# Block-sparse attention for the last two head pairs of a fused attention and gated-MLP kernel, with sampled keys copied by GpSimd and sampled value rows gathered by DMA

## The chip, the cores and the metric

The kernel runs on one core of a Trainium2 chip. The metric is the device time of one execution in microseconds, lower being better. Engines are named as in the profile: PE is TensorE, DVE is VectorE, ACT is ScalarE, POOL is GpSimd, SP is SyncE.

## The reference

BigBird attention over 4 batches, 8 heads, 768 tokens and 64 features, in blocks of 32 tokens (24 blocks), and then a gated MLP over the 512 features of each batch.

```python
mask = np.abs(blk_i - blk_j) <= 1                     # neighbours
mask |= (blk_i == 0) | (blk_j == 0) | (blk_i == 23) | (blk_j == 23)
for qb in range(24):
    for kb in sampled_blocks[qb]:                     # 3 drawn blocks, may repeat
        mask[qb*32:(qb+1)*32, kb*32:(kb+1)*32] = True
attn = softmax(where(mask, q @ k.T / 8, -1e9));  x = attn @ v
...
h = relu(x @ w_in);  u, v = halves of h
v_n = (v - mean(v)) / sqrt(var(v) + 1e-6)
out = (u * (w_spatial @ v_n + b_spatial)) @ w_out     # w_spatial mixes tokens
```

A query block thus attends to at most 8 of the 24 key blocks (itself, its neighbours, the first, the last, three drawn), except the first and last query blocks, which attend to all. The drawn blocks are an input, known only when the kernel runs.

## The kernel before, in words

Heads go in pairs; the four pairs of a batch fill the 128 partitions of four feature tiles. There are 16 pairs, numbered 0 to 15. The work is written out by hand as a sequence of slots, and no scheduler changes the order: every engine executes its instructions in program order. Functions put into a slot by `when` (line 726) are called in the loop at line 846.

Pairs 0 to 3 (batch 0) are treated in thirds in slots 0 to 35. From slot 36 on (`S0`) each head takes six slots and each pair twelve; `slot_of(p)` is the first. Pair 14 begins at slot 156 and pair 15 at 168; the last dense slot is 179.

- **Loads** (`load`, line 106) bring q, k and v of a pair, each partition holding six consecutive tokens, through SyncE's queue. **Casts** (`cast`, line 118) to bf16 are done on GpSimd. **`tr_dma`** (line 373) transposes q and k by a DMA from SyncE, and **`split`** (line 376) copies a head's half into `kq` on VectorE, beside rows that carry the block mask.
- **`qk_full`** (line 421): scores of 128 keys by all 768 queries, two matmuls (512 and 256 columns, line 428) per slot, and one exponential on ScalarE (line 431) into `a_all`. The mask comes in through 24 extra rows of the contraction, so all 24 x 24 blocks are computed.
- **`av_full`** (line 471): seven slots later, six matmuls of 65 columns (line 476) sum value rows of 128 queries; column 65 is the sum of weights. `normalize` (line 438) divides on VectorE.
- **`xtr_dma`** (line 507) transposes a pair's result into `xt`, the input of the MLP. For the last pair `last_x` (line 785) does it on PE, behind all that is left of the MLP of batch 2.

The **MLP** of a batch is cut into 108 steps of about one 512-column matmul (lines 561 and 630). `deal` and `run_queue` spread them evenly over 48 slots; those of batch 2 run in slots 144 to 191, that is beside pairs 13 to 15, and those of batch 3 behind everything. Six v products come first, mixed with the u products: for each, VectorE takes the relu (line 185), the statistics (lines 594 and 595), and after three of them GpSimd works out `std` and `rstd` (lines 598 and 600). Nine or more steps later VectorE normalizes `vn` in place (`vn_one`, line 615, recorded as line 185). From about slot 165 on the spatial products (line 630, `w_spt` by `vn`) read all six `vn`, and VectorE multiplies the result into `un` (lines 661 and 664). PSUM gives the MLP two banks, the scores two tiles and the values two.

SyncE issues every DMA of this stage in program order, output stores among them, and waits at one whose data aren't ready.

## Time and profile before

| | |
|---|---|
| median of 3 runs | 210.07 us (209.88 to 210.24) |
| span of the profiled execution | 208.3 us |
| time of the profiled execution around its span | not given; the median is 1.77 us above the span |
| PE, DVE, ACT, POOL busy | 201.0, 146.8, 168.4, 89.4 us |
| DMA | 39.48 MB, all on hardware queues |

A profile row names line, engine and operation, then the tile written and the tile read, the shape, and how many there were. "PEld" is a weight load. In the grouped view the columns are busy time and mean duration of one in ns, then the idle time ahead of it and who ended it; in the timeline the first two numbers are start and length in us, and the bracket tells idle time ahead and its releaser. Matmuls are pipelined, so durations of single matmuls overlap.

### The profile page before, as it was taken

Reading aid. Unit: us, or ns where it says so; the run is one execution under the profiler, and the core shown is the slowest. Engines: PE = TensorE matmul, PEld = TensorE weight load, DVE = VectorE, ACT = ScalarE, POOL = GpSimd, SP = SyncE. Lnnn points to the kernel's source line nnn. Section 1 sums busy time; section 2 is a strip of 40 time slices with the busy share of each in tenths; the row PEclk is TensorE's granted clock in tenths of the full one; section 3 lists DMA queues with packets and bytes.
Section 4 is the critical chain, followed back from the end, with each engine's and each line's share of the span. In section 5 each row is a group of like instructions: output and inputs, shape, how many; then the busy total and the mean of one; then the engine's idle time right before and its main releaser. Section 6 shows DMA issues by size and latency. Waiting matters only on the chain.

```text
span 208.3 us, 5489 instructions
## 1 busy us (share of the span) xinstructions
PE 201.0 (97%) x2203; PEld 138.0 (66%) x2225; DVE 146.8 (70%) x315; ACT 168.4 (81%) x222; POOL 89.4 (43%) x186
## 2 busy tenths in 40 slices
PE   6899999999999999999999999999999999999993
PEld 6599888777766776667556676667665567445551
DVE  6888776989876766575975585456875666576871
ACT  6899999999999999989899878889899884266021
POOL 6888989767927964006757600006210000013000
PEclk9999999999999999999999999999999999999999
DMA  5999899999999999499987920499402010610016
GB/s 143 338 362 357 275 383 270 206 247 389 253 253 308 259 300 208 139 199 386 292 176 206 139 41 0 164 189 335 75 0 41 0 37 4 250 57 0 0 70 232
DMA packets 53053, 39.48 MB, mean 190 GB/s; under 512 B 33956, under 2 KB 47652, under 8 KB 53028
## 3 DMA queue, kind: packets, MB, share of 16 engines
q1 hardware_dynamic: 52596, 38.74, 70.0%
q10 hardware_dynamic: 432, 0.39, 0.6%
q8 instruction: 17, 0.28, 0.5%
q14 instruction: 8, 0.07, 0.1%
HBM read 24.77 MB, written 6.29 MB: 149 GB/s over the span
## 4 chain that ended last, share of the span: by engine, by line
PE 87%; DVE 4%; ACT 4%; DMA 2%; issue 1%; POOL 0%; ACTq 0%
PE ps L428 21%; PE ps_moe L630 17%; PE ps_moe L561 13%; PE ps_av L476 12%; PE ps L415 7%; PE ps_av L458 4%; PE ps_t L561 4%; PE ps_t L630 4%; PE ps_sc L630 2%; ACT a_all L420 2%; DVE stats L594 2%; DVE vn L185 2%; DMA st_q<-in_q_dram 2%; PE ps_sc L561 1%; PE ps L263 1%
## 5 line engine op out<-in xcount | busy, mean ns | idle before, releaser
L431 ACT ACTIVATE a_all<-ps 128x768 bf16<-128x768 f32 x144 | 113.4, 812 | 13.8 <-PE ps L428 6.2
L428 PE MATMUL ps<-kq 128*128 128x512 bf16 (+1 forms) x288 | 70.3, 326 | 0.3
L476 PEld LDWEIGHTS <-a_all 128*128 128x128 bf16 x864 | 46.6, 98 | 19.0
L476 PE MATMUL ps_av<-vv,a_all 128*128 128x65 bf16 x864 | 51.1, 194 | 0.1
L428 PEld LDWEIGHTS <-kq 128*128 128x128 bf16 x288 | 27.9, 97 | 23.6
L137 POOL CAST nat<-st_k 128x256 bf16<-128x256 f32 (+3 forms) x37 | 17.7, 509 | 38.7 <-DMA st_k<-in_k_dram 38.7
L420 ACT ACTIVATE a_all<-ps 128x1024 bf16<-128x1024 f32 x35 | 33.5, 1027 | 0.3
L630 PE MATMUL ps_moe<-w_spt,vn 128*128 128x512 bf16 (+1 forms) x144 | 33.1, 325 | 0.0
L598 POOL TENSOR_SCALAR std<-mv 128x3 f32<-128x3 f32 (+1 forms) x9 | 3.4, 376 | 48.7 <-DVE mv L595 48.5
L661 DVE TENSOR_TENSOR sb<-ps_moe,b_row 128x512 f32<-128x512 f32 x18 | 12.4, 690 | 14.5 <-PE ps_moe L630 14.2
L630 PE MATMUL ps_moe<-xt,w_in_t 128*128 128x256 bf16 (+1 forms) x108 | 21.7, 299 | 0.2
L415 PE MATMUL ps<-kq 128*128 128x256 bf16 x135 | 20.8, 275 | 0.8 <-DVE kq L211 0.6
L561 PE MATMUL ps_moe<-w_in_t,xt 128*128 128x512 bf16 x65 | 20.2, 378 | 0.2
L137 POOL CAST vv<-st_v 128x256 bf16<-128x256 f32 (+2 forms) x37 | 18.5, 533 | 3.9 <-DMA st_v<-in_v_dram 3.8
L137 POOL CAST nat<-st_q 128x256 bf16<-128x256 f32 (+2 forms) x41 | 19.2, 496 | 1.6 <-DMA st_q<-in_q_dram 1.5
L561 PE MATMUL ps_moe<-w_out_t,un 128*128 128x512 bf16 x64 | 19.4, 378 | 0.2
L441 DVE TENSOR_TENSOR xn<-ps_av,rc 128x384 bf16<-128x384 f32 (+1 forms) x36 | 18.5, 513 | 1.4 <-DVE rc L440 0.2
L664 DVE TENSOR_TENSOR un<-sb,un 128x512 bf16<-128x512 f32 x24 | 17.4, 727 | 1.5
L630 PEld LDWEIGHTS <-vn 128*128 128x128 bf16 x192 | 15.5, 97 | 4.4
L594 DVE BATCH_NORM_STATS2 stats<-vn 128x6 f32<-128x512 bf16 x24 | 16.5, 688 | 1.5 <-ACT vn L589 0.9
L211 DVE COPY osb<-ps_moe 128x512 f32<-128x512 f32 x12 | 8.3, 689 | 11.2 <-PE ps_moe L561 9.3
L211 DVE COPY kq<-tt 64x1536 bf16<-64x1536 bf16 x24 | 15.4, 641 | 0.6 <-DMA tt<-nat 0.2
(94 smaller groups left out, 241.6 us busy)
## 6 DMA issues: line engine op xcount, KB each, us to landing
out_dram<-osb SPq DMA_DIRECT2D x23, 256.0 KB, 2.1
st_k<-in_k_dram SPq DMA_DIRECT2D x15, 384.0 KB, 4.6
st_v<-in_v_dram SPq DMA_DIRECT2D x15, 384.0 KB, 6.2
st_q<-in_q_dram SPq DMA_DIRECT2D x12, 384.0 KB, 4.9
ws_f<-in_moe_w_spatial_dram SPq DMA_DIRECT2D x6, 384.0 KB, 5.5
w_f<-in_moe_w_in_dram SPq DMA_DIRECT2D x8, 256.0 KB, 6.3
w_f<-in_moe_w_out_dram SPq DMA_DIRECT2D x4, 256.0 KB, 5.4
st_q<-in_q_dram SPq DMA_DIRECT2D x3, 256.0 KB, 6.9
```

Source lines behind the costliest of these rows:

```text
L137: eng.tensor_copy(out=dst, in_=src)
L211: nc.vector.tensor_copy(out=o, in_=i)
L415: nc.tensor.matmul(out=ps[:, at:at + n * TW], lhsT=kq[:, h, ci * 128:(ci + 1) * 128], rhs=kq[:, h, qcols(t0, n)], start=True, stop=True)
L420: nc.scalar.activation(out=out, in_=ps, func=AF.Exp, scale=0.125)
L428: nc.tensor.matmul(out=ps[:, n0:n1], lhsT=kq[:, j % H, ci * 128:(ci + 1) * 128], rhs=kq[:, j % H, S + n0:S + n1], start=True, stop=True)
L431: nc.scalar.activation(out=a_ref["h", j][:, ci, :], in_=ps[:, 0:S], func=AF.Exp, scale=0.125)
L441: nc.vector.tensor_tensor(out=out, in0=ps[:, :, 0:D], in1=rc[:, 0:n].to_broadcast([128, n, D]), op=ALU.mult)
L476: nc.tensor.matmul(out=av_ref[j][:, qc, :], lhsT=a_ref["h", j][:, ci, qc * 128:(qc + 1) * 128], rhs=vv[p % NVV][:, h, ci, :], start=(ci == ...
L561: nc.tensor.matmul(out=ref["ps"][:, 0:w], lhsT=lhs(i), rhs=rhs(i), start=(i == 0), stop=(i == n - 1))
L594: nc.vector.bn_stats(out=stats, in_=self.vn[:, tcc, :])
L630: nc.tensor.matmul(out=o.rearrange("p (c t) -> p c t", c=n), lhsT=lhs(i)[:, (d0 + x) * 128:(d0 + x + 1) * 128], rhs=rhs(i), start=(i == 0) ...
L664: nc.vector.tensor_tensor(out=self.in_place(*area), in0=sb, in1=self.in_place(*area), op=ALU.mult)
```

## The change

Pairs 14 and 15 (`PS = NP - 2`) leave the dense path. Line numbers of the changed kernel are given where needed.

**Data.** q, k and v of the two pairs are loaded with token t on partition t mod 128 (runs of 256 bytes, one DMA per head), so that transposed columns are tokens in order. Their bf16 value rows, 260 wide for four heads, are also written to a scratch tensor in memory with 32 zero rows behind them.

**Keys.** For query blocks 3 to 22 two blocks share a chunk "f" of 128 keys: the two blocks themselves, the first and the last. Each query block has a chunk "x": one neighbour outside of the pair, and its three drawn blocks. Blocks 1 and 2 form one more such group, blocks 0 and 23 use all keys ("d"). VectorE copies fixed keys (`k_pairs`, `k_edges`); GpSimd copies drawn ones (`k_sampled`), loading twelve block positions at a time into registers.

**Values.** Fixed rows come by plain DMAs (`v_pairs`); for each x chunk one indirect DMA from GpSimd fetches 128 rows (`v_sampled`). Repeated or already present blocks are pointed at the zero rows, by an index computed on GpSimd (`sample_index`, about 45 small operations).

**Attention.** Per pair 17 score matmuls of 128 columns (chunks f and d, two heads at once) and 22 of 64 (x), nine exponentials, and 78 value matmuls. Weights go into 128x128 tiles that are zero outside the chunk's own queries; VectorE sets `a_cols` to zero once for that (`a_zero`). Queries are turned by 96 tokens (`q_split`), and results turned back by `x_order`. Value matmuls follow scores by four slots in place of seven.

```diff
+    def k_sampled(x0, n):
+        vals = nc.values_load_multi_w_load_instructions(
+            key_at[0:1, x0:x0 + n].rearrange("o n r -> o (n r)"),
+            engines=[mybir.EngineType.Pool], min_val=0, max_val=S - BLK,
+            skip_runtime_bounds_check_because="block numbers")[1]
+        src = kt_cols.rearrange("x (i t) -> x i t", i=2)
+        for j, val in enumerate(vals):
+            x, r = x0 + j // NR, j % NR
+            nc.gpsimd.tensor_copy(out=xk[:, :, x, (r + 1) * BLK:(r + 2) * BLK],
+                                  in_=src[:, :, bass.ds(val, BLK)])
+    def v_sampled(x):
+        nc.gpsimd.indirect_dma_start(
+            out=vx(x), out_offset=None, in_=rows_of_v,
+            in_offset=bass.IndirectOffsetOnAxis(ap=row_at[:, x:x + 1], axis=0))
+    def a_zero(n, eng):
+        eng.memset(a_cols[:, n * AW:min((n + 1) * AW, A_END)].bitcast(FP32), 0.0)
+    def q_split(i, h, copy):
+        rs = slice(h * D, (h + 1) * D)
+        src = tt["q"].rearrange("x c n -> x (c n)")[rs, i * S:(i + 1) * S]
+        copy(q2[i][rs, h, 0:S - QR], src[:, QR:S])
+        copy(q2[i][rs, h, S - QR:S], src[:, 0:QR])
+    def scores(ps, at, i, kind, n):
...
+        w = BLK if kind == "x" else 2 * BLK
+        nc.tensor.matmul(out=ps[:, at:at + 2 * w].rearrange("p (h t) -> p h t", h=2),
+                         lhsT=lhs, rhs=q2[i][:, :, t0:t0 + w], start=True, stop=True)
...
-    for p in range(NG, NP):
+    for p in range(NG, PS):
...
+    T = slot_of(PS)
+    when(70, samples)
...
+    for i in range(80, 100):
+        when(i, lambda: [todo.pop(0)() for _ in range(min(2, len(todo)))])
+    when(100, zero_rows)
+    when(101, v_ones, c(q_zero, 0), c(q_zero, 1))
+    for nm, p, ld, ca in (("v", 14, 110, 122), ("v", 15, 114, 124), ("k", 14, 116, 127),
+                          ("k", 15, 118, 129), ("q", 14, 126, 138), ("q", 15, 136, 146)):
+        when(ld, c(load, p, nm))
+        when(ca, c(cast, p, nm, PL))
+    when(126, v_out)
+    when(131, c(tr_group, "k"))
+    when(134, v_pairs)
+    for i in range(2):
+        when(136 + i, c(k_edges, i, dve_copy))
+        when(140 + 2 * i, c(k_pairs, i, dve_copy))
+    for x in range(NX):
+        when(134 + x, c(v_sampled, x))
+    for j in range(6):
+        when(137 + 3 * j, c(k_sampled, 4 * j, 4 if j < 5 else 2))
+    when(148, c(tr_group, "q"))
+    for i in range(2):
+        for h in range(2):
+            when(152 + 4 * i + h, c(q_split, i, h, dve_copy))
+    when(T - 5, c(a_zero, 0, nc.vector))
+    when(T + 2, c(a_zero, 1, nc.vector))
+    when(T + 7, c(a_zero, 2, nc.vector))
...
-    for s in range(NS + LAG + 2):
+    for s in range(NS + LAG):
```

In the slots, `samples` and the index operations (two a slot) come early, then four fills of 64x768 on GpSimd (`q_zero`), 22 gathers, 66 copies in six groups, and the three fills `a_zero` of 2304, 2304 and 384 words on VectorE; `T` is slot 156.

The `tr_dma` and `split` calls of pairs 14 and 15 are gone, with their four copies of 64x1536 on VectorE. `last_x` moves from slot 188 to 186; its two copies on VectorE become one there and two on ScalarE. The MLP's staging tiles `osb` go from 6 to 5, and several tiles now share one space. In GpSimd's program order the gathers and copies stand in six groups, each of three or so gathers and up to twelve copies; the two query casts lie behind the first and the third group, and the first `std` and `rstd` of batch 2 stand behind 19 of the gathers and all 66 copies. In VectorE's order the first normalization of `vn` stands ahead of the last `q_split`, two v products and two of the three `a_zero`.

327 lines of the change are left out of this document (302 added, 25 removed).

## The prediction

> **What bounds the kernel now.** I read the page first, for which engine is full, then the chain, then the stage that the change touches.
>
> ```profile
> span 208.3 us, 5489 instructions
> PE 201.0 (97%) x2203; PEld 138.0 (66%) x2225; DVE 146.8 (70%) x315; ACT 168.4 (81%) x222; POOL 89.4 (43%) x186
> ...
> PEclk9999999999999999999999999999999999999999
> ...
> PE 87%; DVE 4%; ACT 4%; DMA 2%; issue 1%; POOL 0%; ACTq 0%
> ```
>
> TensorE is busy 97% of the span at full clock and makes 87% of the chain. Busy time of PE counts pipelined matmuls too long, so I took the cost of one from the chain where dense slots are over and only values (L476) and projections remain, and the length of a slot from the exponentials, one per slot (columns: minimum, median, maximum in ns; first and last start).
>
> ```profile
> 175.37 0.43 PE ps_moe L561 x2
> 175.80 0.19 PE ps_av L476 x6
> 175.99 0.43 PE ps_moe L561 x2
> ```
> ```profile
> L431 ACT ACTIVATE a_all<-ps x54: 804/812/831, 120.1 to 173.1; 128x768 bf16<-128x768 f32 x54
> ```
>
> Two 512-column matmuls take 0.43 us, 0.42 ns a column; six 65-column ones 0.19, 0.031 each. The slot is (173.1 - 120.1) / 53 = 1.00 us: 768 columns of scores 0.324, values 0.19, and 108 projection steps over 48 slots at 0.216, that is 0.486. The sum is 1.00, so PE has no air and every column removed is worth time, if the others keep up. The exponential (0.81) fits inside. The last dense slot starts at 172.3, so slot s starts at 149.3 + 1.00 (s - 156), and slots 156 to 179 are the last two pairs.
>
> The other engines there, by stage:
>
> ```profile
> core 0: us, PE busy (x) PEld busy (x) DVE busy (x) ACT busy (x) POOL busy (x), PEclk, DMA share, GB/s
> ...
> 130.00:135.00 5.00, 4.95 (x54) 3.03 (x52) 2.09 (x5) 4.38 (x8) 0.00 (x0) 1.00 0.43 156
> ...
> 145.00:150.00 5.00, 4.95 (x57) 3.05 (x55) 3.78 (x8) 4.30 (x6) 1.47 (x2) 1.00 0.62 103
> 150.00:155.00 5.00, 4.95 (x55) 3.04 (x55) 4.74 (x12) 4.48 (x7) 0.00 (x0) 1.00 0.00 0
> 155.00:160.00 5.00, 4.95 (x52) 2.93 (x50) 3.12 (x9) 4.92 (x8) 1.12 (x2) 1.00 0.20 39
> ```
>
> GpSimd is idle from 119 to 141 us, and VectorE is nearly full from 150 to 155: batch 2's six v products go through its relu, statistics and normalization there.
>
> **The change, part by part.**
>
> *TensorE.* A pair's 12 dense slots cost 12 x 0.324 = 3.89 us of scores and 72 x 0.031 = 2.23 of values. The new form has 17 matmuls of 128 columns (0.054 each by columns) and 22 of 64 (no cheaper than a 65-column one, 0.031): 1.60 us; values are 78 matmuls, 2.42. So 2.1 us a pair, 4.2 for both, 0.175 a slot. That is the whole gain; ACT's smaller exponentials bring nothing, as ACT is not the limit. The new reordering copies on ACT lie in slots where exponentials have become smaller, so I cost them at nothing; uncovered they would be some 1 us.
>
> *GpSimd.* New there: about 45 tiny index operations and four 64x768 fills, in slots 80 to 101; then 22 gathers and 66 copies at a register's address, behind 6 register loads. In program order the statistics of batch 2 (std, rstd) now stand behind 19 gathers and all 66 copies. Before:
>
> ```profile
> 141.16 1.09 POOL L137 CAST nat<-st_k 128x256 bf16<-128x256 f32 x3 [21.77 <-DMA st_k<-in_k_dram]
> ...
> 148.35 0.59 POOL L598 TENSOR_SCALAR std<-mv 128x3 f32<-128x3 f32 x1 [3.82 <-DVE mv L595]
> 149.02 0.88 POOL L600 TENSOR_TENSOR rstd<-std,mhalf 128x3 f32<-128x3 f32 x1
> ```
>
> The chain starts when the transposed keys land. SyncE can issue that transpose behind pair 10's output transpose:
>
> ```profile
> 121.49 1.21 SPq L508 DMA_TRANSPOSE xt<-xn  x1
> ...
> 135.23 1.47 SPq L374 DMA_TRANSPOSE tt<-nat  x1
> 136.75 0.87 SPq L109 DMA_DIRECT2D st_k<-in_k_dram  x1
> 137.67 0.86 SPq L109 DMA_DIRECT2D st_q<-in_q_dram  x1
> 138.57 0.47 SPq L109 DMA_DIRECT2D st_v<-in_v_dram  x1
> ```
> ```profile
> DMA to landing us min/median/max: 4.0/5.2/9.3
> ```
>
> 122.7 + 5.2 (median landing of tt<-nat) = 127.9 us. Four gathers are done by then, as their rows of V are in memory earlier and their space is free from slot 125. Behind that, up to the statistics: 66 copies, 6 loads, 15 gathers, two query casts of 128x768.
>
> ```profile
> L137 POOL CAST nat<-st_q 128x768 bf16<-128x768 f32 x2 | 1.7, 828 | 0.3 <-DMA st_q<-in_q_dram 0.3
> ...
> L162 POOL IOTA hot<- 64x768 bf16 x1 | 0.8, 791 | 0.0
> ...
> L137 POOL CAST nat<-st_k 128x128 bf16<-128x128 f32 x1 | 0.3, 291 | 0.0
> ```
> ```profile
> out_dram<-osb SPq DMA_DIRECT2D x23, 256.0 KB, 2.1
> ```
> ```profile
> L171 POOL MEMSET vv<- x6: 148/180/206, 2.7 to 3.0; 128x12 bf16 x6
> ```
>
> ```profile
> 100.20 0.59 POOL L598 TENSOR_SCALAR std<-mv 128x3 f32<-128x3 f32 x1 [3.17 <-DVE mv L595]
> ```
>
> The four fills of 64x768, 0.8 us each by the iota of that size, may hold batch 1's statistics by up to 1 us; I take 0, as GpSimd waited 3.17 us ahead of those.
>
> No GpSimd DMA, register load or register address is in this trace. A *gather* I bound by what an issue holds SyncE: 0.47 (the cheapest load) to 1.47 us (a transpose, the kind that is more than a plain list). I take 0.85, nearest to the two other loads. A *copy* of 64 elements lies between 0.06 (spacing of the small fills: 0.3 us over 5) and 0.29 (128 elements). I take 0.15: 64 elements at the three casts' 1.09 us / 768 are 0.09, and 0.06 for the instruction that works out the address. A *register load*: between a small fill's 0.18 and the 2.1 us of an output store's way to memory; I take 0.5, as nothing leaves the chip's core. Sum: 15 x 0.85 + 66 x 0.15 + 6 x 0.5 + 1.7 = 27.4 us, so the statistics run at 155.3, and rstd is there at 156.8 instead of 149.9.
>
> *Queries.* They are cast behind 8 gathers and 3 groups: 127.9 + 6.8 + 5.4 + 1.5 + 1.7 = 143.3, transposed by 148.5, split by VectorE with a v product between the halves at about 151. Slot 156 wants them at 149.3, a stall of 1.7 us that the next one contains.
>
> *VectorE.* In order, it stands at the first normalization until rstd comes. Behind that it has six normalizations, two v products, two fills of the weight buffer, one query split and two xn normalizations. Before:
>
> ```profile
> 144.99 0.54 DVE L211 COPY kq<-tt 64x1536 bf16<-64x1536 bf16 x1
> ...
> 150.98 0.73 DVE L185 TENSOR_SCALAR vn<-vn,mv,rstd 128x512 bf16<-128x512 bf16 x2
> 151.79 0.69 DVE L185 TENSOR_SCALAR vn<-ps_moe 128x512 bf16<-128x512 f32 x1
> 152.52 0.69 DVE L594 BATCH_NORM_STATS2 stats<-vn 128x6 f32<-128x512 bf16 x1
> 153.25 0.18 DVE L595 BATCH_NORM_AGGREGATE mv<-stats 128x2 f32<-128x6 f32 x1
> ...
> 156.54 0.56 DVE L441 TENSOR_TENSOR xn<-ps_av,rc 128x384 bf16<-128x384 f32 x1
> ...
> 158.81 0.41 DVE L185 TENSOR_SCALAR vn<-vn,mv,rstd 128x512 bf16<-128x512 bf16 x1
> 161.70 0.69 DVE L661 TENSOR_TENSOR sb<-ps_moe,b_row 128x512 f32<-128x512 f32 x1 [2.49 <-PE ps_moe L630]
> ```
>
> Its length: 6 x 0.40 + 2 x 1.56 + 2 x 0.75 + split 0.46 = 7.5 us, and the fills, whose rate no row shows: 2304 words at the 1.0 ns of a 512-word copy below is 2.4 us, at the bf16 copies' 0.35 ns (0.54 us for 1536) 0.8. I take 2.4, and 0.4 for the small one: 10.3 us.
>
> ```profile
> L211 DVE COPY b_row<-b_nat x2: 378/499/620, 52.8 to 53.1; 128x256 f32<-128x256 f32 x1, 128x512 f32<-128x512 f32 x1
> ```
>
> So the last vn is ready at 156.8 + 10.3 = 167.1 instead of 159.2, 7.9 us later. The spatial products begin in slot 165 and read every vn, so PE waits for it; what it saved up to there is lost, and 15 slots x 0.175 = 2.6 us are still saved behind it. Net 7.9 - 2.6 = +5.3: span 213.6. The key copies on VectorE (14, some 2.7 us at 0.35 ns and 0.08 each) lie in 129 to 136, where it is busy 2.09 us in 5; uncovered they cost that much.
>
> *Total.* The profiled run's time outside its span isn't given; the median 210.07 is 1.77 above the span. 213.6 + 1.77 = **215.4 us**.
>
> The Trainium skill, "DMA: Bandwidth & Descriptors", section "Latency and other measured facts", gives about 1 us for the first byte of a DMA whose descriptors GpSimd makes, and about 600 ns as the floor of a register load. No run here shows either; read as GpSimd's time for one, the sum would be 15.0 + 9.9 + 3.6 + 1.7 = 30.2 us, an estimate from that page, and the total 218.2.
>
> **The rivals.**
>
> *GpSimd keeps up; VectorE sets the end.* This is the faster side. With gathers at 0.47, copies at 0.06 and loads at 0.18 the chain is 13.8 us, ends at 142, and nobody waits. The bound is then VectorE: it gains 1.8 us of query splits (8 copies, 3072 columns) and 2.0 to 5.2 of fills, loses four kq splits (2.2), net 1.6 to 4.8. From 145 to 160 it was idle 15 - 3.78 - 4.74 - 3.12 = 3.4 us, 0.8 of it behind the last vn. So that vn is 0 to 2.2 us late, and the result 2.6 to 0.4 us faster: 207.5 to 209.7. The point from which it decides is a chain of 22 us (22 + 127.9 + 1.5 + 10.3 - 159.2 - 2.6 = 0): gathers of 0.5 us at my other prices, or of 0.7 with copies of 0.10. For it: all three prices are bounds from other engines and operations. Against: only the lowest price of a gather reaches it, and the chain has no idle time that could be used up first.
>
> *GpSimd slowed by VectorE.* The same three casts take 1.09 us, and 1.64 beside a VectorE product of two SBUF operands:
>
> ```profile
> 114.02 1.64 POOL L137 CAST nat<-st_k 128x256 bf16<-128x256 f32 x3 [1.50 <-DMA st_k<-in_k_dram]
> 115.60 1.09 POOL L137 CAST nat<-st_q 128x256 bf16<-128x256 f32 x3
> ```
> ```profile
> 114.35 0.69 DVE L664 TENSOR_TENSOR un<-sb,un 128x512 bf16<-128x512 f32 x1
> ```
>
> If the whole chain stretched by that 1.5, 27.4 becomes 41 and the end moves 13.7 us on, to 229. Against: VectorE stands still during its own wait, so the stretch would cease. The Trainium skill, "SBUF — State Buffer", section "Who interferes with whom", says that the two share a port pair, held for a whole instruction by whoever starts first. By that rule descriptor making is held up too; the stretched row agrees with it.
>
> *The work isn't removed.* Excluded: the changed program has 240 dense score matmuls where 288 stood, and 78 small ones.
>
> **How the numbers follow.** Forecast (GpSimd late, 210.5 to 222): 0.59. GpSimd keeps up (206 to 210.5): 0.30, of which 0.25 lie below 209.65 and 0.05 within 0.2%. Slowed, or dear gathers (222 to 235): 0.11. The range that leaves out 2 in 10: 207.3 to 223.5; its low end is the first rival's whole gain, its high end gathers of 1.4 us (15 x 0.55 = 8.2 more). The forecast's own range is 210.5 to 222. Faster by over 0.2%: 0.25; within 0.2%, about what a measurement of this kernel can tell from no change: 0.05; slower: 0.70.
>
> **What would show it.** Right: std of batch 2 starts after 153 us with GpSimd without a gap from 128 on; VectorE's longest wait is vn for rstd; PE has gaps of microseconds near 155 to 168 and none elsewhere. Each gather's spacing between 0.7 and 1.1 us, each copy near 0.15. Wrong: std at 148 to 150 with idle ahead of it, or PE at 99% through 150 to 168, or a kernel that loses its time before 128 us, which nothing here forecasts.

## The result, and the profile after

The changed kernel takes 230.7 us (median of four, 228.0 to 232.4) where the kernel before takes 210.1: a ratio of 1.0895, 95% interval 1.0851 to 1.0938. Two of the four executions, 231.7 and 232.4 us, were in a slower state with a lower granted clock, so the ratio, and what the edits below gain, are counted from the other two, 228.9 us on average. The forecast was 215.4 with a range up to 223.5. The direction was right, the size was not.

The profiled execution took 231.69 us; a second trace of the same kernel (below), of an execution of 230.05 us, has the same waits. The page of the first:

```profile
span 229.8 us, 5957 instructions
...
PE 205.1 (89%) x2267; PEld 138.6 (60%) x2267; DVE 154.0 (67%) x335; ACT 159.5 (69%) x220; POOL 134.1 (58%) x304
...
PEclk9999999999999999999799999999965999999999
...
PE 63%; POOL 16%; issue 6%; DVE 5%; DMA 4%; ACT 3%; POOLq 1%; SPq 0%; ACTq 0%; DVEq 0%
```

TensorE went from 97% to 89% busy, its clock has two dips, and GpSimd holds 16% of the chain where it had none. The same windows of both kernels tell where (columns: window, its length, busy time of PE, PEld, DVE, ACT and POOL, granted clock, DMA share, GB/s). Before:

```profile
95.00:125.00 30.00, 29.84 (x318) 19.23 (x319) 21.14 (x43) 26.30 (x37) 15.76 (x37) 1.00 0.81 199
125.00:153.00 28.00, 27.73 (x298) 18.15 (x301) 17.87 (x37) 24.78 (x34) 4.71 (x11) 1.00 0.56 142
153.00:185.00 32.00, 31.84 (x316) 19.59 (x316) 19.68 (x41) 21.42 (x31) 1.12 (x2) 1.00 0.20 63
```

After:

```profile
95.00:125.00 30.00, 26.83 (x263) 16.08 (x261) 17.52 (x35) 22.28 (x31) 19.44 (x41) 0.94 1.05 235
125.00:153.00 28.00, 24.89 (x270) 16.36 (x267) 18.04 (x42) 19.72 (x27) 21.26 (x50) 1.00 0.67 157
153.00:185.00 32.00, 20.56 (x245) 12.60 (x242) 18.42 (x39) 13.01 (x23) 17.52 (x44) 0.84 0.25 47
```

TensorE's idle time rose by 3.0, 2.8 and 11.3 us. To this comes what the clock costs while TensorE works at 0.5 of its speed (below). There are three losses, then.

**Between 95 and 125 us**, GpSimd's timeline (start, duration, line, shape; in brackets the idle time ahead and what ended it):

```profile
98.16 0.30 POOL L639 MEMSET ws<- 32x260 bf16 x1
102.99 0.21 POOL L643 MEMSET ws<- 128x24 bf16 x1 [4.53 <-DMA v_rows<-ws]
103.03 1.56 POOL L707 MEMSET oh<- 64x768 bf16 x2
...
106.22 0.25 POOL L930 TENSOR_SCALAR std<-mv 128x3 f32<-128x3 f32 x1
```

`zero_rows` takes its zeros from a piece of `ws` that the ones of `v_ones` overwrite. So the fill at 643 waits 4.53 us for the store of the zeros, and batch 1's statistics, queued behind it, run at 106.2 instead of 100.2. TensorE stands 2.97 us, at 109.0, for the normalization that needs them.

**Between 125 and 153 us** TensorE has gaps that no releaser explains (below, "what stays open"). **Behind 153** comes the wait that the prediction was about. Two kinds of rows out of GpSimd's queue, and its end:

```profile
130.85 0.94 POOL L659 DMA_INDIRECT kq<-v_rows,row_at  x1 [0.30 <-issue]
132.10 0.94 POOL L659 DMA_INDIRECT kq<-v_rows,row_at  x1 [0.30 <-issue]
133.92 2.66 POOL L694 COPY ws<-kt 128x64 bf16 x12 [0.88 <-issue]
...
165.66 1.11 POOL L694 COPY ws<-kt 128x64 bf16 x6
166.86 0.24 POOL L930 TENSOR_SCALAR std<-mv 128x3 f32<-128x3 f32 x1
167.19 0.89 POOL L932 TENSOR_TENSOR rstd<-std,mhalf 128x3 f32<-128x3 f32 x1
```

A gather is 0.94 us busy and 1.25 us from the next, a copy 2.66 / 12 = 0.22 us. The statistics start at 166.9, rstd is there at 168.1. And what that holds up, on all engines:

```profile
168.12 0.41 DVE L220 TENSOR_SCALAR vn<-vn,mv,rstd 128x512 bf16<-128x512 bf16 x1 [5.29 <-POOL rstd L932]
...
171.56 1.98 DVE L736 MEMSET a_all<- 128x2304 f32 x1 [0.43 <-issue]
...
173.63 0.60 ACT L777 ACTIVATE a_all<-ps 128x512 bf16<-128x512 f32 x1 [10.97 <-DVE a_all L736]
...
174.28 0.59 PE L746 MATMUL ps<-oh,ws 128*128 128x64 bf16 x8 [10.00 <-ACT a_all L777]
...
179.16 0.20 DVE L479 RECIPROCAL rc<-ps_av 128x6 f32<-128x6 f32 x1 [3.94 <-PE ps_av L515]
...
182.29 0.40 DVE L220 TENSOR_SCALAR vn<-vn,mv,rstd 128x512 bf16<-128x512 bf16 x1
```

Read from below. TensorE waits 10.0 us for ScalarE to empty a score buffer; ScalarE waits 10.97 us for the second fill of the weight buffer (`a_zero`, line 736); that fill stands in VectorE's queue behind a normalization that waits for rstd. The fill depends on nothing that GpSimd makes. It is only queued behind something that does.

The clock, in windows set around that wait (same columns):

```profile
168.10:174.20 6.10, 0.00 (x0) 0.00 (x0) 5.56 (x10) 0.57 (x1) 3.13 (x3) 0.52 0.14 33
174.20:178.30 4.10, 4.02 (x40) 2.63 (x40) 0.96 (x3) 0.94 (x3) 1.13 (x2) 0.50 0.00 0
178.40:182.00 3.60, 3.60 (x56) 2.49 (x55) 1.97 (x7) 2.46 (x7) 0.00 (x0) 0.98 0.44 41
```

TensorE comes back at 174.3 to half its clock and gets the rest 4.1 us later. Some 2 us of work are lost by that, and VectorE's 3.94 us wait at 179.16 is an echo of it. The Trainium skill, "TensorE: Matmul & The Clock Gate", section "What's actually happening", says that the clock is halved after an idle window of about 3.4 us and restored after a busy one. The trace agrees: after its last work at 164.3 the granted clock is still full up to 168, half from 168.3 on, and full again some 4 us after TensorE's return.

### The profile page after: what moved, and what is told of

Same layout as the page of the kernel before. It is cut to its first block, busy times and chain, and to the rows that moved or that the text cites. A ratio compares the mean times of both kernels' runs of the same rounds, so it can differ in the third digit from the quotient of the medians.

```text
span 229.8 us, 5957 instructions
## 1 busy us (share of the span) xinstructions
PE 205.1 (89%) x2267; PEld 138.6 (60%) x2267; DVE 154.0 (67%) x335; ACT 159.5 (69%) x220; POOL 134.1 (58%) x304
## 3 DMA queue, kind: packets, MB, share of 16 engines
q0 software_dynamic: 704, 1.47, 2.8%
## 4 chain that ended last, share of the span: by engine, by line
PE 63%; POOL 16%; issue 6%; DVE 5%; DMA 4%; ACT 3%; POOLq 1%; SPq 0%; ACTq 0%; DVEq 0%
PE ps_moe L962 14%; PE ps L467 10%; PE ps_moe L893 6%; PE ps L455 6%; PE ps_av L515 5%; PE ps_av L497 4%; PE ps_t L893 4%; PE ps_t L962 3%; POOL ws L694 3%; DMA ws<-in_sampled_blocks_dram 2%; POOL ws L659 2%; POOL ws L598 2%; PE ps_sc L962 2%; PE ps_av L815 2%; DMA v_rows<-ws 2%
## 5 line engine op out<-in xcount | busy, mean ns | idle before, releaser
L470 ACT ACTIVATE a_all<-ps 128x768 bf16<-128x768 f32 x120 | 93.5, 812 | 20.9 <-PE ps L467 9.9
L467 PE MATMUL ps<-kq 128*128 128x512 bf16 x240 | 59.2, 329 | 3.4 <-ACT a_all L470 2.1
L515 PEld LDWEIGHTS <-a_all 128*128 128x128 bf16 x720 | 39.1, 99 | 15.3 <-issue 0.6
L515 PE MATMUL ps_av<-vv,a_all 128*128 128x65 bf16 x720 | 43.1, 195 | 0.0
L467 PEld LDWEIGHTS <-kq 128*128 128x128 bf16 x240 | 23.4, 98 | 24.7 <-issue 7.6
L962 PE MATMUL ps_moe<-xt,w_in_t 128*128 128x256 bf16 (+1 forms) x112 | 24.9, 320 | 3.7 <-DVE vn L220 3.7
L455 PE MATMUL ps<-kq 128*128 128x256 bf16 (+1 forms) x136 | 21.0, 275 | 0.8 <-DVE kq L246 0.7
L220 DVE TENSOR_SCALAR vn<-vn,mv,rstd 128x512 bf16<-128x512 bf16 x24 | 10.5, 462 | 12.3 <-POOL rstd L932 12.2
L479 DVE RECIPROCAL rc<-ps_av 128x6 f32<-128x6 f32 (+1 forms) x36 | 6.6, 183 | 17.6 <-PE ps_av L515 9.6
L172 POOL CAST vv<-st_v 128x256 bf16<-128x256 f32 (+2 forms) x31 | 16.2, 552 | 1.7 <-DMA st_v<-in_v_dram 1.6
```

The source lines that it names most:

```text
L172: eng.tensor_copy(out=dst, in_=src)
L455: nc.tensor.matmul(out=ps[:, at:at + n * TW], lhsT=kq[:, h, ci * 128:(ci + 1) * 128], rhs=kq[:, h, qcols(t0, n)], start=True, stop=True)
L467: nc.tensor.matmul(out=ps[:, n0:n1], lhsT=kq[:, j % H, ci * 128:(ci + 1) * 128], rhs=kq[:, j % H, S + n0:S + n1], start=True, stop=True)
L470: nc.scalar.activation(out=a_ref["h", j][:, ci, :], in_=ps[:, 0:S], func=AF.Exp, scale=0.125)
L515: nc.tensor.matmul(out=av_ref[j][:, qc, :], lhsT=a_ref["h", j][:, ci, qc * 128:(qc + 1) * 128], rhs=vv[p % NVV][:, h, ci, :], start=(ci == ...
L962: nc.tensor.matmul(out=o.rearrange("p (c t) -> p c t", c=n), lhsT=lhs(i)[:, (d0 + x) * 128:(d0 + x + 1) * 128], rhs=rhs(i), start=(i == 0) ...
```

## The experiments

The theory after the result: GpSimd's queue (gathers dearer than assumed) holds back batch 2's rstd, VectorE and TensorE wait in turn, and the wait for the zero rows adds 5 us. The rivals: VectorE is full there whatever GpSimd does; or the transfers themselves, not the order, cost the time. Line numbers shift by a few where an edit adds lines. The diffs are cut to the lines that matter: what an earlier one shows is named in words and not printed again. Times are medians; beside each, the kernel before took 209.9 to 210.3.

### Own zero rows

```diff
+    zeros = const.tile([BLK, VW], BF16, name="zeros")
-        z = ws_cols[0:BLK, WS3:WS3 + VW]
-        nc.gpsimd.memset(z, 0.0)
-        nc.sync.dma_start(out=rows_of_v[S:S + BLK], in_=z)
+        nc.gpsimd.memset(zeros, 0.0)
+        nc.sync.dma_start(out=rows_of_v[S:S + BLK], in_=zeros)
```

> The zero rows that the masked samples read are written from a tile of their own, so the fill of the ones (GpSimd, line 643 of the changed kernel) no longer waits for their store. Nothing else changes, and the output is the same. Theory (the first 5 us, between 100 and 112 us, are this wait alone: 4.53 us of GpSimd idle ahead of the fill, and batch 1's rstd 5.6 us later than before): the time falls by 4.5 to 5.5 us, to 224-226 us where the changed kernel has 228-231, and everything behind is the same but 5 us sooner. Rival (the end is set by the GpSimd chain of batch 2 whatever comes ahead of it, and that chain starts with the loads): the 5 us come back as a longer wait later, and the time falls by under 2 us.

227.5 us (226.4 to 228.1), ratio 1.0811 (1.0766 to 1.0855). GpSimd's timeline:

```profile
98.71 0.30 POOL L640 MEMSET zeros<- 32x260 bf16 x1
98.96 0.19 POOL L644 MEMSET ws<- 128x24 bf16 x1
...
102.51 0.25 POOL L931 TENSOR_SCALAR std<-mv 128x3 f32<-128x3 f32 x1
```

The wait is gone, and TensorE is busy 30.00 us of the 30 from 95 to 125, although the four fills still put the statistics 2.3 us later than before. The time fell by some 1.5 us only, counted from 228.9: that is the rival's "under 2", not the theory's 4.5. The first gather came 1.6 us sooner (126.3) and rstd 3.9 us (164.2), and the long wait at the fill shrank only from 10.0 to 9.2 us. Ahead of it a new stop took the rest back:

```profile
153.45 0.42 DVE L246 COPY oh<-tt 64x672 bf16<-64x672 bf16 x2 [5.48 <-DMA tt<-nat]
...
154.52 0.59 PE L963 MATMUL ps_moe<-xt,w_in_t 128*128 128x512 bf16 x1 [5.56 <-DVE vn L220]
```

VectorE waits for a transposed block of queries, and TensorE stands 5.56 us for the work queued on VectorE behind it. The cast that the transpose needs is in GpSimd's queue behind gathers and runs at 148.2. In the changed kernel the same stop, at 158.5, was 0.5 us. So GpSimd's queue holds up two things that TensorE needs, not one.

### Fixed rows instead of the gathers

```diff
-        when(134 + x, c(v_sampled, x))
+    def fixed_rows():
+        for to in (vx_a, vx_b):
+            nc.sync.dma_start(out=to, in_=rows_of_v[0:128, None, :].to_broadcast([128, to.shape[1], VW]))
+    when(134, fixed_rows)
```

> The 22 gathers on GpSimd's queue are replaced by two plain transfers on SyncE's queue, which write the same places with as many bytes (the first 128 rows of v, repeated), so the sampled value rows are left out of the result; the 66 copies of keys stay. GpSimd's chain loses 22 x 1.25 = 27.5 us of its 39. Theory (GpSimd's chain up to batch 2's rstd is most of the loss): rstd of batch 2 comes at 155 to 158 us instead of 168.1, the query casts 10 us sooner, TensorE's clock does not fall at 170-180 us, and the time falls by 10 to 13 us, to 216-220 us. On the gaps of TensorE without a releaser at 132-155 us (4.3 us in all): if GpSimd's descriptors or its queue make them they go as well, if it is the bytes that the DMA engines move they stay, and the time is at the upper end. Rival (VectorE's own work behind the norm sets the end): rstd is sooner, but the last normalisation of batch 2 only by 2 or 3 us, and the time falls by under 4 us.

220.8 us (220.3 to 222.4). rstd at 157.6, as expected, but some 8 us won, not 10 to 13. GpSimd now waits 4.47 us for the statistics' input, so it isn't the bound any more, and TensorE still stands 4.8 us at the fill. The gaps that no releaser explains are gone from 125 to 153 us (TensorE's longest stop there is 1.8 us, for a transpose). By the expectation that speaks against the bytes that are moved; but the kernel above and the next one lose them with their gathers in place, so this run alone doesn't show it.

### Fixed keys instead of the copies

```diff
-        when(137 + 3 * j, c(k_sampled, 4 * j, 4 if j < 5 else 2))
+    def fixed_keys(i):
+        nc.vector.tensor_copy(out=xk[:, i, :, BLK:4 * BLK],
+                              in_=kt(i)[:, None, 0:3 * BLK].to_broadcast([128, NX, 3 * BLK]))
+    for i in range(2):
+        when(138 + i, c(fixed_keys, i))
```

> The 66 copies of keys on GpSimd and the loads of their registers are replaced by two copies of a fixed block of keys on VectorE at slots 138 and 139 (some 2 us each, where VectorE is about 0.6 busy), so the sampled keys are left out of the result; the 22 gathers stay on GpSimd. GpSimd's chain loses 13 us of its 39. Theory (GpSimd's chain): batch 2's rstd comes near 155 us instead of 168.1, and the time falls by 8 to 12 us, less up to 2 if VectorE's two copies delay the normalisation, to 218-223 us; the gaps without a releaser at 132-155 us stay, since they began with the gathers. Rival (VectorE sets the end): the time falls by under 3 us, or rises by the two copies.

218.3 us (217.9 to 219.7), rstd at 153.8: some 10.5 us won, as expected (8 to 12). Contrary to the expectation the gaps at 125 to 153 us went too. What is left is one wait (times in all, how often, longest):

```profile
ACT a_all L777 <- DVE a_all L736: 6.0, 1, 6.0
...
PE ps L746 <- ACT a_all L777: 5.1, 1, 5.1
```

and VectorE's timeline shows what the fill stands behind:

```profile
153.73 0.41 DVE L246 COPY st_q<-tt 64x672 bf16<-64x672 bf16 x2
154.07 0.40 DVE L220 TENSOR_SCALAR vn<-vn,mv,rstd 128x512 bf16<-128x512 bf16 x1
...
155.20 0.41 DVE L220 TENSOR_SCALAR vn<-vn,mv,rstd 128x512 bf16<-128x512 bf16 x1
...
157.58 1.98 DVE L736 MEMSET a_all<- 128x2304 f32 x1 [0.43 <-issue]
```

With rstd early, VectorE's own order is the next bound: splits that nobody needs for ten slots stand ahead of a fill that TensorE needs at once.

### All three edits

Own zero rows, fixed rows and fixed keys in one kernel:

```diff
+        nc.gpsimd.memset(zeros, 0.0)
-        when(134 + x, c(v_sampled, x))
+    when(134, fixed_rows)
-        when(137 + 3 * j, c(k_sampled, 4 * j, 4 if j < 5 else 2))
+        when(138 + i, c(fixed_keys, i))
```

> The three edits together: zero rows from a tile of their own, fixed value rows by SyncE in place of the gathers, fixed keys by VectorE in place of the copies; sampled keys and rows are left out of the result. GpSimd has the casts, the fills and the norm alone. Theory (the loss is GpSimd's chain plus the wait for the zero rows; TensorE's saved work is worth some 4 us at its slot): the time comes to 207-212 us, about that of the kernel before, 210.1, and TensorE is busy over 95% of the span. Rival (VectorE with its fills, splits and copies, not GpSimd, is the bound of the last stage): 213-218 us with VectorE's idle share near zero between 150 and 175 us. Second rival (the transfers of rows hold up instruction streams): gaps without a releaser of 3 us or more stay between 125 and 155 us.

221.8 us (218.5 to 222.6), above both theory and rivals, with a wait that the edit itself seems to make. In its waits from 136 to 150 us:

```profile
PE ps_moe L894 <- DMA xt<-xn: 3.5, 1, 3.5
```

The wait is for the transpose of a pair's result, which stands on SyncE's queue behind the two large row transfers (they take that queue from 128.6 to 131.2 us); that these make it late is argued from its place in the queue, and no run isolates it. The 4.8 us at the fill are still there (rstd at 157.9). So this run doesn't test the sum; a later one avoids the transfers.

### The changed kernel again

The file is the changed kernel's own, with no edit.

> The changed kernel as it is, for a second trace. In its first trace TensorE and ScalarE have gaps at 132-155 us that no releaser explains (4.3 us in all), while the kernels with own zero rows, or with fixed keys, hardly have them although their gathers are the same. Theory: the gaps belong to that one execution and are no part of the change; here the offset of TensorE's scores against the kernel before stays at 1 to 5 us from slot 116 to slot 152, and the time is 228 to 230 us. Rival: they come of the gathers or of the row transfers and are there again, 3 us or more between 130 and 155 us.

230.05 us, span 228.1. The gaps between 125 and 153 us are there again (PE busy 24.59 of 28 us, first trace 24.89), so they belong to the kernel, as the rival had it.

### Eleven gathers behind the norm

```diff
-        when(134 + x, c(v_sampled, x))
+        when(134 + x if x < 11 else 153 + (x - 11) // 2, c(v_sampled, x))
```

> Zero rows from a tile of their own, and of the 22 gathers the last 11 stand behind batch 2's std and rstd on GpSimd's queue (slots 153 to 158 in place of 145 to 155); nothing is left out. GpSimd has 11 x 1.25 us less ahead of the norm, 8 gathers fewer than with own zero rows alone, where rstd came at 164.2 us. Theory (GpSimd's queue holds back rstd, and VectorE, waiting for rstd, holds back its fill of the second third of the probabilities, for which ScalarE and then TensorE wait): rstd comes at 153 to 156 us, the wait of ScalarE for the fill shrinks from 10.2 us to about 6 as in the run with fixed keys, and the time falls from 227.5 to 216-220 us, if the late gathers are there before their value products. Rival (the copies and gathers are waited for themselves): the products wait for late rows or keys, and the time stays above 223 us.

Nothing is left out here, and with own zero rows the time is 224.3 us (223.3 to 224.3), above the expected 216 to 220. rstd came at 156.1 and the wait for the fill was 5.0 us, as expected. It is the best time of the whole computation here. But TensorE has gaps from 125 to 153 us (24.66 of 28 busy), the longest of which began in ScalarE and VectorE:

```profile
132.47 0.60 ACT L249 ACTIVATE osb<-ps_moe 128x512 f32<-128x512 f32 x1 [2.84 <-remote]
132.71 0.69 DVE L246 COPY osb<-ps_moe 128x512 f32<-128x512 f32 x1 [2.75 <-remote]
...
133.81 0.48 PE L467 MATMUL ps<-kq 128*128 128x512 bf16 x2 [2.96 <-ACT a_all L470]
```

"Remote" is an event that no instruction of this trace is known to have sent. The run with own zero rows has the same instructions and tiles up to slot 145, behind this place, was made on the same chip, and has no such stop.

### The fill in pieces, and ahead

The reordered fills, beside own zero rows and fixed keys:

```diff
-    when(T + 2, c(a_zero, 1, nc.vector))
+    when(T + 1, c(a_fill, AW, 4 * QW, nc.vector))
+    when(T + 3, c(a_fill, 4 * QW, 2 * AW, nc.vector))
-            when(152 + 4 * i + h, c(q_split, i, h, dve_copy))
+            when(152 + 9 * i + h, c(q_split, i, h, dve_copy))
```

> Zero rows from a tile of their own, fixed keys by VectorE in place of the 66 copies (the sampled keys are left out of the result), and VectorE's work at the change of the stage reordered: the second fill is cut in two, the 1536 columns that the next exponentials need first (slot 157, some 0.7 us in place of 1.98 us at slot 158), the other 3072 at slot 159, and the four splits of the last pair's queries stand at slots 161 and 162 instead of 156 and 157. Theory (VectorE's fill, behind its splits and its norm, is what TensorE waits for at 155-160 us, 5.1 us in the run with fixed keys, and the lower clock behind it costs 2 to 3 us more): the wait falls under 1.5 us, the clock stays over 0.95, and the time is 210-212.5 us, where that run had 218.3. Rival (VectorE is full there, and the wait only moves to the vn of batch 2): 215 us or more.

232.7 us (229.1 to 233.4), some 20 above the theory. The wait at the fill is gone as expected (TensorE's longest for ScalarE's sparse exponentials is 0.99 us), but from 125 to 153 us:

```profile
125.00:153.00 28.00, 15.99 (x128) 8.92 (x128) 8.08 (x21) 9.19 (x12) 20.13 (x21) 0.69 0.59 135
```

128 matmuls where the kernel before ran 298. From the run with fixed keys, made on the same chip, only the moment at which the zero rows were stored differs ahead of that stretch, and the places in memory of the tiles behind the new one; the reordered instructions come later than the gaps, which begin at 131 us. ScalarE and VectorE stop here too, for up to 4.9 and 5.5 us, again at events called remote.

The second kernel leaves nothing out:

```diff
+        nc.gpsimd.memset(zeros, 0.0)
-        when(134 + x, c(v_sampled, x))
+        when(134 + x if x < 11 else 153 + (x - 11) // 2, c(v_sampled, x))
-    when(T + 2, c(a_zero, 1, nc.vector))
+    when(T + 1, c(a_fill, AW, 4 * QW, nc.vector))
+    when(T + 3, c(a_fill, 4 * QW, 2 * AW, nc.vector))
```

> The whole computation: own zero rows, the last 11 gathers behind batch 2's norm, and the fill cut in two with the splits of the last pair later. Theory: GpSimd's queue and VectorE's fill are the two waits that make the loss, so without both the time comes to 210-214 us, near the kernel before (210.3), and TensorE saves at its slots what it lost in waits. Rival (the late gathers, or the copies that still take 13 us of GpSimd, become the wait): 215-221 us with TensorE waiting for ws or kq rows at 158-172 us.

The whole computation with own zero rows, late gathers and the reordered fills: 228.1 us (227.2 to 229.0), again above theory and rival. While the 11 late gathers run, 157.7 to 171.2 us, TensorE stops every few instructions, in front of instructions for which the trace names no releaser:

```profile
167.04 0.19 PE L750 MATMUL ps<-oh,ws 128*128 128x64 bf16 x1 [0.50 <-issue]
...
172.00 0.22 PE L819 MATMUL ps_av<-kq,a_all 128*128 128x65 bf16 x1 [1.77 <-issue]
```

### No gathers, no other transfer

Own zero rows, fixed keys and reordered fills as above, and the rows filled on GpSimd. The diff is against the fixed rows:

```diff
-            nc.sync.dma_start(out=to, in_=rows_of_v[0:128, None, :].to_broadcast([128, to.shape[1], VW]))
+            nc.gpsimd.memset(to.rearrange("p n w -> p (n w)").bitcast(FP32), 0.0)
```

> As the run with fixed keys and the reordered fills, and the 22 gathers replaced by two fills with zeros on GpSimd (some 3 us each, slot 134), so sampled keys and sampled rows are both left out of the result, and no transfer takes the gathers' place. Theory (the loss is the wait for the zero rows, GpSimd's queue ahead of batch 2's rstd, VectorE's fill and the clock behind each stall): none of the four is left, TensorE has no gap over 1 us between 100 and 185 us, its clock stays at 1.00, and the time is 206-210 us, under the kernel before by what TensorE is spared, which the traces so far put at 1 to 3 us. Rival (VectorE is full behind the change of stage): 212 us or more. And the run tells what the gathers cost by themselves in the reordered kernel, 232.7 us with them.

210.7 us (210.2 to 212.6), ratio 1.0041 (1.0017 to 1.0064). Its page and its window from 125 to 153 us:

```profile
PE 199.1 (95%) x2245; PEld 137.1 (65%) x2267; DVE 155.1 (74%) x338; ACT 159.8 (76%) x220; POOL 102.6 (49%) x218
...
PEclk9999999999999999999999999999999999999999
```
```profile
125.00:153.00 28.00, 27.55 (x304) 18.20 (x308) 22.18 (x52) 24.29 (x34) 5.87 (x6) 1.00 0.61 141
153.00:185.00 32.00, 28.73 (x356) 18.39 (x358) 22.44 (x46) 13.04 (x28) 1.24 (x2) 1.00 0.25 63
```

Without the wait for the zero rows, the gathers, the copies and the late fill TensorE has no gap over 1.5 us, the clock stays full, and some 18 us of the changed kernel's time are gone. With the gathers both their length on GpSimd's queue and their price for TensorE have gone, so this run doesn't separate these two. Against the run of 232.7 us only the gathers are missing (two fills of 1.4 and 1.2 us stand in their place): there, 22 gathers cost some 20 to 22 us, although the trace shows no instruction that waits for one.

```diff
-        when(138 + i, c(fixed_keys, i))
+        when(137 + 3 * j, c(k_sampled, 4 * j, 4 if j < 5 else 2))
```

> The same with the 66 real copies of keys on GpSimd in place of VectorE's two, so only the sampled rows are left out of the result (zeros). Theory: 13 us of copies, alone on GpSimd's queue from 131 us, end at 150 us at the latest, before batch 2's rstd is due, and cost nothing: within 1.5 us of the run without them, 206-211 us. Rival (the copies slow VectorE or TensorE beside them): 3 us or more above it.

With the 66 real copies: 211.0 us (210.6 to 212.3). They take 0.18 to 0.23 us each, end at 145 us, and cost nothing.

### What in the gathers costs TensorE its time

```diff
-        nc.gpsimd.indirect_dma_start(out=vx(x), out_offset=None, in_=rows_of_v, in_offset=...)
+        nc.gpsimd.dma_start(out=vx(x), in_=rows_of_v[x * BLK:x * BLK + 128])
```

> As the run with fixed keys and the reordered fills, but the 22 gathers are 22 plain transfers of 128 rows from fixed places, on the same queue of GpSimd; sampled keys and rows are left out of the result. In that run with the gathers TensorE has gaps that no wait explains from 131 to 157 us (12 us in all), during the gathers, and the clock at 0.5 behind them. If it is the indirect form (rows by index) that makes them, they go, and the time is 207-213 us; if it is GpSimd's software queue, or its spacing, they stay, and the time is 222-233 us. If neither, and the gaps come by chance of the moment, the rounds differ among themselves by over 3 us.

The four times are 211.6, 217.7, 211.5 and 219.1 us: two as without gathers, two 7 to 8 us above. The expectation had named a spread of over 3 us as the sign of chance, so the plain form isn't cleared by this run; its trace is of the first execution, without the loss. On GpSimd (columns: shortest, median, longest in ns) the plain form takes

```profile
L660 POOL DMA_DIRECT2D kq<-v_rows x12: 544/544/816, 125.0 to 132.7; - x12
```

and the indirect one, in the changed kernel,

```profile
L659 POOL DMA_INDIRECT kq<-v_rows,row_at x12: 940/946/1434, 127.9 to 151.1; - x12
```

```diff
-        do(gs, row_at, n[:, :, 0], 1.0, ALU.mult)
+        do(iota, e[:, :, 0], [[BLK, NX]], 0, 1)
+        do(gs, row_at, e[:, :, 0], 1.0, ALU.mult)
```

> As the run of 232.7 us (own zero rows, fixed keys, reordered fills, 22 gathers), with one difference: the gathers' row numbers are 32x + p for gather x and partition p, so they read the rows that the 22 plain transfers of the run of 214.6 us read, through the indirect form. Sampled keys and rows are left out of the result. If the rows that are read (scattered, or many the same zero rows) make TensorE's unexplained gaps, they go and the time is 210-217 us as with plain transfers. If it is the indirect form, with its 1.25 us per gather on GpSimd, they stay: 224-236 us.

Indirect, but reading the plain form's rows: 232.4 us (230.0 to 234.1): all four above all four of the plain form. So it isn't the rows that are read, and the indirect form is the dearer one.

```diff
+    when(134, c(b_fill, NX - XA))
-        when(134 + x, c(v_sampled, x))
+        if x < XA:
+            when(134 + x, c(v_sampled, x))
```

> As the run of 232.7 us, with the first 12 of the 22 gathers (those that write into kq) and zeros by one fill on GpSimd for the other ten. Sampled keys and ten of 22 blocks of sampled rows are left out of the result. If the gaps grow with the number of gathers (a price per gather), about 12/22 of the 22 us that gathers cost there: 220-225 us. If it takes a long row of gathers, or the gathers that write into ws: 211-215 us.

Twelve gathers: 221.3 us (220.5 to 223.2), 10.6 above none, where 22 cost 20 to 22. The price goes with the number, 0.9 to 1.0 us of the kernel's time for each.

```diff
         if x < XA:
             when(134 + x, c(v_sampled, x))
+            when(134 + x, c(b_fill, XA // 2))
```

> The same 12 gathers, each followed on GpSimd by a fill of 1.3 us or more of the part of ws that no gather writes (zeros again), so that they come 2.5 us apart or more instead of 1.25. If it is the density of gathers that makes TensorE's gaps: 210.5-214 us, and less than the run with 12 gathers in a row by 3 us or more. If each gather has its price whatever its spacing: the same as that run within 2 us.

The same twelve, 1.9 to 3.1 us apart: 219.8 us (217.7 to 221.4). By the time spacing is worth 1.6 us, but the trace says that it is worth more. The added fills, 0.76 us each, hold up a cast of queries on GpSimd (152.1 us, 141.9 without them), and TensorE waits for it:

```profile
156.79 0.42 DVE L246 COPY oh<-tt 64x672 bf16<-64x672 bf16 x2 [3.86 <-DMA tt<-nat]
...
157.86 0.58 PE L966 MATMUL ps_moe<-xt,w_in_t 128*128 128x512 bf16 x1 [3.94 <-DVE vn L220]
```

From 125 to 153 us, where the gathers run, TensorE is busy 25.2 us with the spaced ones, 21.7 with the row of twelve and 27.6 with none. There spacing cuts what the gathers cost from 5.9 to 2.3 us, so how close they stand does count.

Own zero rows and fixed keys, without the reordered fills:

```diff
+        nc.gpsimd.memset(zeros, 0.0)
+        nc.sync.dma_start(out=rows_of_v[S:S + BLK], in_=zeros)
-        when(137 + 3 * j, c(k_sampled, 4 * j, 4 if j < 5 else 2))
+        when(138 + i, c(fixed_keys, i))
```

> Own zero rows and fixed keys, with the gathers and with VectorE's fills and splits as in the changed kernel (the sampled keys are left out of the result): one edit less than the run of 232.7 us, one more than the run with fixed keys alone, 218.3 us. Theory (VectorE's fill costs the 5 us stall at 155 us, the reorder is not what brought the gaps at 131-157 us): 216-218 us if the gaps stay away as with fixed keys alone; 228 us or more if the sooner start of the row stores is what brings them.

236.3 us (233.2 to 237.8), where fixed keys alone took 218.3. The two kernels have the same gathers in the same order. Their windows from 125 to 153 us, fixed keys alone first:

```profile
125.00:153.00 28.00, 27.78 (x310) 18.16 (x308) 23.09 (x51) 24.06 (x34) 22.08 (x23) 1.00 0.81 184
```
```profile
125.00:153.00 28.00, 13.68 (x117) 7.73 (x118) 7.98 (x21) 8.76 (x12) 20.24 (x21) 0.76 0.64 132
```

GpSimd's columns are alike; TensorE's are 310 matmuls against 117.

Fixed keys and reordered fills, with the zeros in `ws` as in the changed kernel. The diff is against the run of 232.7 us:

```diff
-    zeros = const.tile([BLK, VW], BF16, name="zeros")
-        nc.gpsimd.memset(zeros, 0.0)
+        z = ws_cols[0:BLK, WS3:WS3 + VW]
+        nc.gpsimd.memset(z, 0.0)
-        nc.sync.dma_start(out=rows_of_v[S:S + BLK], in_=zeros)
+        nc.sync.dma_start(out=rows_of_v[S:S + BLK], in_=z)
```

> Fixed keys (the sampled keys are left out of the result) and the reordered fills, with all 22 gathers, and the zero rows written from ws as in the changed kernel: the run of 232.7 us without its own tile for the zero rows, or the run of 218.3 us with the reordered fills. If the gathers' price for TensorE belongs to the kernels with the tile of their own (218.3 us had none of it, 236.3 us with the tile had all of it), it stays away, the 5 us stall at the fill goes too, and the time is 210-213 us. If it comes with any change of order, 225 us or more.

233.2 us (232.4 to 235.5): the price is there without the zero rows' own tile. Up to slot 156 this kernel has the instructions and the tiles of the run of 218.3 us, and its gaps begin long before that, at 133.6 us. It was made on another chip than the run of 218.3 us.

Fixed keys alone, and a tile that nothing uses:

```diff
+    zeros = const.tile([BLK, VW], BF16, name="zeros")
```

> Fixed keys, the zero rows written from ws as in the changed kernel, and a tile of 520 bytes a partition that nothing uses, so that everything allocated behind it lies where it lies in the run of 236.3 us; no instruction differs from the run of 218.3 us but in addresses. If the places in memory are what makes the gathers dear for TensorE, 228-237 us. If it is the moment at which the gathers run beside other transfers, 217-220 us.

236.2 us (234.5 to 242.4): the instructions of the run of 218.3 us, with other addresses. By the expectation it is the places in memory. But the run just above has the price at the addresses of the run of 218.3 us, so they don't explain it alone. Nor does the chip: the run of 232.7 us was made on the chip of the runs of 218.3 and 227.5 us, the only ones whose gathers cost nothing in that stretch, and so was the one of 224.3 us, which has the gap at 132 us with the addresses and instructions of the run of 227.5. The runs of 218.3 and 227.5 us were made together, some 20 minutes before those two, and it can be that the price differs from one occasion to the next.

Late gathers and reordered fills, with the zeros in `ws`:

```diff
-        when(134 + x, c(v_sampled, x))
+        when(134 + x if x < 11 else 153 + (x - 11) // 2, c(v_sampled, x))
-            when(152 + 4 * i + h, c(q_split, i, h, dve_copy))
+            when(152 + 9 * i + h, c(q_split, i, h, dve_copy))
```

> The whole computation, zero rows written from ws, the last 11 gathers behind batch 2's norm, reordered fills: the run of 228.1 us without its own tile for the zero rows. If the tile brings the gathers' price, 5 us for the wait for the zero rows come back and the price goes: 213-220 us. If not, 228-234 us.

229.9 us (226.9 to 231.7), the whole computation once more: no order tried here brings it near the kernel before; the best was 224.3 us.

**What stays open:** why indirect gathers stop TensorE, and ScalarE and VectorE with it, for up to 1 us each in most runs and not in two. The rows that are read are excluded. The spacing is not, it counts; transfers on GpSimd's queue as such are not either, since the plain form cost nothing in two executions and 7 to 8 us in two. Neither the addresses nor the chip explains it alone. In the changed kernel itself, where copies stand between groups of mostly three or four gathers, it is the smaller part: some 3 us of gaps in both traces.

## Why the prediction was wrong, point by point

**The step that failed** is the sum "15 x 0.85 + 66 x 0.15 + 6 x 0.5 + 1.7 = 27.4 us, so the statistics run at 155.3". Counted from the first gather at 127.87 to the statistics at 166.86 it was 39.0: the gathers, the copies and the time of the start were put too low. By terms:

| term | forecast | measured | error |
|---|---|---|---|
| 15 gathers | 0.85 each | 1.25 apart | +6.0 |
| the start: "four gathers are done by then" | 0 | 4 x 1.25 | +5.0 |
| 66 copies | 0.15 each | 13.2 in all, 0.20 each | +3.3 |
| 6 register loads | 3.0 | at most 0.9, ahead of the first group | -2.1 |
| 2 casts | 1.7 | 1.65 | 0 |

The errors come to +12.2 and the difference is 11.6. The gather's price was bounded by issues on SyncE; the range of 0.47 to 1.47 held it, the value "nearest to the two other loads" didn't. With the measured spacing alone the same sum would have given 215.4 + 6.0 = 221.4. The five us of the start have two causes, either of which would do alone. The first four gathers were not done ahead: the first ran at 127.87, behind the store of the rows of v that had been issued at 122.11. And the keys were not there at 127.9: their transpose was issued at 127.78 (forecast 122.7), and the same one took 4.9 to 5.6 us from issue to landing in three other runs, which puts the keys at 132.7 or later, when the four gathers, done at 133.0, were just over. The 0.9 us ahead of the first copies may be the loads or the wait for these keys; ahead of the other five groups there is no such time. Of the Trainium skill's figures quoted there ("DMA: Bandwidth & Descriptors", section "Latency and other measured facts") the 1 us was nearer to 1.25 than my 0.85; the 600 ns for a register load, which no row shows six times, was too much, as my 0.5 was.

**VectorE behind rstd** was forecast at 10.3 us and took 14.6 (168.1 to 182.7). The fills were dearer in the forecast (2.4) than in the trace (1.98); the excess is 3.94 us of waiting for a TensorE at half clock, which no step had. Put together: rstd 11.3 us later than forecast and VectorE 4.3 longer make 213.6 + 15.6 = 229.2, and the span is 229.8. The agreement is luck in its last step, as the next point shows. Right was that GpSimd's chain sets batch 2's rstd and that VectorE and TensorE wait for it in turn; wrong were the sizes in that chain, and the place at which TensorE stops.

**Where TensorE stops** was wrong: the forecast had it wait for the last vn at the spatial products, and it stopped six slots sooner at the fill, for 10.0 us. For the last vn it never waited: the spatial products began at 181.7, before that vn was done at 182.7. So the path by which the forecast's sum reaches the end isn't the one that the kernel took. The fills were counted as length of VectorE's queue and not as something waited for. That is why the rival "GpSimd keeps up" was priced too low, at 207.5 to 209.7: with rstd at 153.8 the kernel still lost 5 us there, and with the fill put right, and without the gathers, it came to 211.0, not below 210.

**TensorE's saving** of 4.2 us: its busy time fell from 201.0 to 199.1 in the run without gathers, and the 3.3 us that it idles there from 153 to 185 us (0.2 before) eat that. How much of the missing 2.3 us is drained pipelines between short groups was only argued.

**The q fills at 0** were right: with own zero rows the statistics are 2.3 us late and TensorE idles nowhere there. The wait that cost 3.0 us at that place was another, between two lines of the diff that touch one piece of `ws`; the prediction didn't ask who still reads a place that a new fill overwrites. The loss ahead of 128 us and TensorE's gaps at 107 to 111 and from 132 on are signs of being wrong that the prediction had named. **The queries** were split at 157.4 instead of 151; TensorE's stop for them was 0.5 us, the rest contained in the next, as forecast. That hung on the long wait behind it: with own zero rows the stop was 5.56 us. **Slowed by VectorE** (229) met the time by another mechanism: a group of 12 copies took 2.16 to 2.95 us, not 1.5 times as long throughout, and the Trainium skill's rule of the shared port ("SBUF — State Buffer", section "Who interferes with whom") isn't needed for the sum.

## What to carry to other kernels

In a kernel ordered by hand, list for every engine what stands behind an instruction that will wait, and move ahead what doesn't need that wait: here a fill and two splits cost 5 us behind nothing, and 10 behind a late rstd. Before a new operation goes onto an idle engine, measure its spacing, not its busy time, and let nothing that the bound engine waits for stand behind a long row of them. And when a change writes into shared space, ask of each new write who reads that place last.

## What the runs showed of the hardware that was not expected

- An indirect DMA of 128 rows of 520 bytes holds GpSimd 0.94 us and comes every 1.25 us; a plain one of the same rows 0.54. A copy of 64 elements a partition at a register's address takes 0.18 to 0.25 us.
- An idle TensorE loses half its clock: a gap of 5.1 us was followed by 0.5 for 4.5 us of work, gaps of up to 1.4 us, in the run of 210.7 us, by none:

```profile
160.30:164.80 4.50, 4.50 (x47) 3.10 (x47) 0.88 (x3) 1.20 (x2) 1.13 (x2) 0.50 0.00 0
164.80:170.00 5.20, 5.20 (x79) 3.60 (x77) 3.02 (x9) 2.96 (x8) 0.00 (x0) 0.98 0.27 41
```

  These are windows of the run with fixed keys: 47 matmuls in 4.5 us, then 79 in 5.2.
- Indirect gathers stopped TensorE, and with it ScalarE and VectorE, by 0.9 to 1.0 us of the kernel's time each where they came in a long row, without a wait for them that the trace shows. Spaced 1.9 to 3.1 us apart they cost TensorE less than half as much in their stretch (2.3 us for twelve, 5.9 in a row). In one long row (218.3 us) and one kernel with groups (227.5 us) they cost nothing there.
